# Softmax sums from a ones column beside each head's values, values loaded in single transfers, and an earlier rank for the splits of the normalised tile, in a one-core attention and two-layer MLP kernel

## The chip, the cores and the metric

One core of one Trainium2 chip runs the whole program in one launch. The metric is device microseconds (us), median of three runs. TensorE is called PE, VectorE DVE, ScalarE ACT, GpSimd POOL, and SP is the engine that issues most transfers.

## What is computed

The reference, cut to its steps (4 batches, 8 heads, 576 positions, 64 per head; 2304 tokens of 512 after the heads are joined):

```python
scores = scale * q @ k.T                       # causal window of 64 positions
attn = softmax(where(mask, scores, -1e9))
x = (attn @ v) joined over heads               # 2304 x 512
xn = x / rms(x) * rms_g
x = (silu(xn @ w_gate) * (xn @ w_val)) @ w_out # d_ff 1536
out = relu(x @ w_in)**2 @ w_out2               # d_ff 2048
```

## The kernel before

**Tiles.** The 2304 tokens are 36 blocks of 64 query positions, 9 to a batch. Block n looks at its own 64 keys and at the 64 before it. Heads go in four pairs, so a block's scores are four 128 x 128 tiles: on the partitions two heads' 64 queries, along the row 128 keys.

**Steps of a block** (`attention` and `block`). PE makes the scores (L430). DVE adds the mask and takes the row minimum (L435). ACT takes the exponential and, in the same instruction, the sum of each row (L437, `accum_out`). DVE turns the sum into its reciprocal (`den` L438, `rs` L439). PE transposes the four tiles into one PSUM bank (L443), ACT or DVE copies them to SBUF (`pt`), PE multiplies with the values (L453) into half of bank 7, DVE scales by `rs` into `acc` (L458), and ACT or DVE squares the result for the norm (L463 on ACT, L465 on DVE). Blocks go through in twos from the fifth on.

**Norm** (`rms`, once per four blocks). PE sums the squares (L479), a chain of nine tiny DVE instructions takes the reciprocal root, and for each block DVE scales `acc` into `xw` (L502), PE turns it by two transposes into half of bank 3 (L506), ACT or DVE copies the turned tile to the high part `xh` (a cast) and DVE takes the low part `xl` (L239, `R<-ps,R`). Copy and subtraction together are called the split of the tile here.

**Products.** All large products use high and low parts of both sides, so each is a run of matmuls at L608, L610 and L612. In the first stage the results go round a ring of three PSUM banks (`mm_ring`, banks 0 to 2), 256 columns each: two for the gate and value products of a feature group, four for the product that goes down. The second MLP (from 545 us, L820 and L884) works on its own banks. Weights arrive as 64-bit numbers and are decoded on ACT and DVE (L555 to L564).

**What sets the order.** Every step is handed to a list (`Schedule.add`) with its engine or two possible engines, a planned cost and a rank. `issue` goes through planned time and gives each engine, among the steps that are ready, the one of lowest rank. A step without a rank takes the lowest rank of what depends on it. A step with two engines goes to the second one only if that would end before the backlog of the first. Where PE's plan has a gap ahead of the first product, small filler matmuls are put in (`keep_busy`, L1015). The engines then run what stands in their queues, in that order, held only by semaphores; these are set per PSUM bank, not per half of a bank.

Of the kernel before, what the change touches and what calls it, by code (L numbers as in the profile page):

```python
# [9 lines left out]
F32 = mybir.dt.float32  # L10
# [6 lines left out]
ALU = mybir.AluOpType  # L17
# [28 lines left out]
PLACE = [5, 6, 1, 7, 2, 3, 4, 0, 8]  # L46
PN = 288
HALVES = 2
NPAIR = DFF2 // (2 * P)
# [4 lines left out]
ILEAD, ISTEP = 8.0, 2.0  # L54
ELEAD = 10.0
PORT, SHARED = 0.8, 1.0

class Schedule:
# [35 lines left out]
    def issue(self):  # L94
# [32 lines left out]
        for _ in range(n):  # L127
            skip = {}
            while True:
# [98 lines left out]
def attn_moe_moe2(ctx: ExitStack, tc: tile.TileContext, qT, kT, vw, w1, w2, w3, w4, rms_g, out):  # L228
# [78 lines left out]
    ps = [psum.tile([P, 512], F32, name=f"ps{i}") for i in range(8)]  # L307
    mm_ring = Ring([0, 1, 2])

# [11 lines left out]
    k_ring = ring(ap, "k", 2, [P, NP, (KB + 1) * WIN])  # L321
    v_ring = ring(ap, "v", 4, [P, DM])
# [3 lines left out]
    small = {k: ring(ap, k, 4, [P, NP]) for k in ("nb", "sum", "den", "rs")}  # L326
# [15 lines left out]
    def setup():  # L342
# [35 lines left out]

    k_tile = {}

    def load_keys(b, m, rank):

        k = k_ring.next()
        k0, k1 = max(KB * m - 1, 0) * WIN, KB * (m + 1) * WIN
        k_tile[b, m] = k, k0
        cuts = (0, WIN, 2 * WIN, k1) if (b, m) == (0, 0) else (k0, k1)
        for c0, c1 in zip(cuts, cuts[1:]):
            at("sp", 0.1 + (c1 - c0) / 110, lambda c0=c0, c1=c1: (nc.scalar if c0 < k0 + WIN and m == b == 0 else nc.sync).dma_start(out=T[k][:, :, c0 - k0 : c1 - k0], in_=kT[b, :, :, c0:c1]), w=[(k, c // WIN) for c in range(c0 - k0, c1 - k0, WIN)], lag=2.0)

    def attention(blocks, rank):  # L390

        todo = [block(n, rank, *more) for n, *more in blocks]
        for step in zip(*todo):
            if step[0][0] == "pe":

                costs, turn, fns, r, w, late = zip(*(x[1:] for x in step))
                at("pe", sum(costs) + turn[0], lambda fns=fns: [fn() for fn in fns], r=sum(r, []), w=sum(w, []), rank=rank + late[0])
            else:
                for x in step:
                    x[1]()  # L400

    def block(n, rank, part, pos):

        nk = WIN if n % NB == 0 else 2 * WIN
        b, i = divmod(n, NB)
        q, v, sm, pt = (r.next() for r in (q_ring, v_ring, sm_ring, pt_ring))
        nb, su, den, rs = (small[i].next() for i in ("nb", "sum", "den", "rs"))
        at("sp", 0.6, lambda: nc.sync.dma_start(out=T[q], in_=qT[n]), w=[q], lag=2.0)
        if i % KB == 0:
            load_keys(b, i // KB, rank)  # L410
        at("sp", 0.75, lambda: nc.sync.dma_start(out=T[v], in_=vw[n]), w=[v], lag=2.0)
        k, k0 = k_tile[b, i // KB]
        k0 = max(i - 1, 0) * WIN - k0
        keys_ = T[k][:, :, k0 : k0 + nk]
        kk = [(k, c // WIN) for c in range(k0, k0 + nk, WIN)]
        par = n % 2
# [3 lines left out]
        t_ps = ps[T_BANK].rearrange("p (a k) -> p a k", a=NP)  # L420
        x_ps = ps[X_BANK].rearrange("p (e a k) -> p e a k", e=2, a=NP)[:, par]
        sk = [("ps", c, par) for c in S_BANKS]
        xk = ("ps", X_BANK, par)

# [7 lines left out]
        def softmax():  # L432
# [15 lines left out]
        def pv():  # L448
            for i in range(2):
                for j in range(2):  # L450
                    for h in range(2):
                        f = (2 * i + h) * 2 * D + j * D
                        nc.tensor.matmul(x_ps[64 * h : 64 * h + 64, 2 * i + j], T[pt][:nk, 2 * i + j, 64 * h : 64 * h + 64], T[v][:nk, f : f + D], start=True, stop=True)  # L453
# [14 lines left out]

        return ("pe", 0.45, 0.28, scores, [q] + kk, sk, 0.0), ("", softmax), ("pe", 0.46, 0.24, pv, [v, pt], [xk], 0.02), ("", result)

# [3 lines left out]
    def rms(t, rank, part):  # L474
# [19 lines left out]
        for i, n in enumerate(blks(t)):  # L494
# [35 lines left out]
    def decode(srcs, rank=None, after=()):  # L530
# [9 lines left out]
        for z, src in zip(raws, srcs):  # L540
            sc.add("sp", 2.4 if closed2 else 1.5, lambda z=z, src=src: nc.sync.dma_start(out=T[z], in_=src), w=[z], lag=2.2, rank=rank, after=after)
        part = lambda i: T[raw].rearrange("p (a b) -> p a b", b=2)[:, :, i]
# [478 lines left out]
    def record(k):  # L1021
# [158 lines left out]
```

## Time and profile before

| | |
|---|---|
| median of three runs | 914.86 us (913.35 to 915.72) |
| the profiled execution's own time | 914.39 us |
| its span, first to last instruction | 912.70 us |
| PE busy | 894.8 us (98% of the span) |
| DVE, ACT, POOL busy | 698.0 (76%), 573.1 (63%), 42.7 us (5%) |
| granted PE clock | 1.0 of full speed (2.4 GHz) in every slice |

The profiled execution is 1.69 us longer than its span, and 0.47 us under the median. Shares over the whole span mix three stages: attention beside the first products (to about 114 us), products alone, and the second MLP.

### The profile page before, as it was taken

To read this page: it belongs to the slowest core of one execution; us is meant where nothing else is said; L and a number is where in the kernel's file an instruction comes from. 1 tells how busy PE (TensorE), PEld (TensorE's weight loads), DVE (VectorE), ACT (ScalarE), POOL (GpSimd) and SP (SyncE) were. 2 spreads that over 40 slices of the span, in tenths; PEclk is the share of its full clock that TensorE was granted. 3 is DMA by queue.
4 is the path that set the end of the run, shared out by engine and by line. 5 is a ranking of instruction groups with operands and counts; after the bars stand their busy time and mean duration, and the time that the engine had idled before them with its cause. 6 is when DMAs were issued, how large, how long until landed. Compare 5 with 4: busy or idle time off the path is not lost.

```text
span 912.7 us, 17324 instructions
## 1 busy us (share of the span) xinstructions
PE 894.8 (98%) x6598; PEld 839.3 (92%) x6598; DVE 698.0 (76%) x1663; ACT 573.1 (63%) x1227; POOL 42.7 (5%) x45
## 2 busy tenths in 40 slices
PE   7889999999999999999999999999999999999997
PEld 6778899989988988988988999999999999999997
DVE  5999987677767877777768558667789976777786
ACT  6998875666666667666667556655557655555561
POOL 1000000000000100000000000000002300000011
PEclk9999999999999999999999999999999999999999
DMA  8856520246535735534556136272717373718142
GB/s 248 267 180 216 164 87 2 93 163 240 181 109 179 239 124 179 204 113 169 189 199 231 56 115 211 79 249 75 267 57 270 106 269 107 274 51 288 36 169 98
DMA packets 67203, 149.50 MB, mean 164 GB/s; under 512 B 6704, under 2 KB 25136, under 8 KB 67120
## 3 DMA queue, kind: packets, MB, share of 16 engines
q1 hardware_dynamic: 66592, 148.26, 47.6%
q8 instruction: 52, 0.85, 0.4%
q14 instruction: 31, 0.25, 0.1%
q10 hardware_dynamic: 528, 0.13, 0.1%
HBM read 114.30 MB, written 34.08 MB: 163 GB/s over the span
## 4 chain that ended last, share of the span: by engine, by line
PE 86%; DVE 11%; DMA 1%; ACT 1%; issue 1%
PE ps L884 19%; PE ps L820 18%; PE ps L608 15%; PE ps L610 15%; PE ps L612 15%; DVE sm L435 2%; DVE R L239 1%; DVE Q L239 1%; DVE xw L502 1%; PE ps L453 1%; DVE acc L458 1%; PE ps L430 1%; PE ps L443 1%; PE ps L1015 1%; DMA Q<-w 1%
## 5 line engine op out<-in xcount | busy, mean ns | idle before, releaser
L820 PE MATMUL ps<-R 128*128 128x288 f32 x1344 | 187.5, 296 | 0.8 <-DVE ps L238 0.6
L820 PEld LDWEIGHTS ps<-R 128*128 128x128 f32 x1344 | 181.6, 189 | 1.8 <-DVE ps L238 0.8
L884 PE MATMUL ps<-L,R 128*128 128x288 f32 x630 | 169.7, 297 | 1.5 <-DVE acc L892 1.3
L884 PE MATMUL ps<-Q,L 128*128 128x288 f32 x480 | 133.4, 297 | 0.0
L884 PEld LDWEIGHTS ps<-L,R 128*128 128x128 f32 x630 | 118.6, 188 | 2.5 <-DVE acc L892 2.0
L608 PE MATMUL ps<-R 128*128 128x256 f32 (+3 forms) x444 | 99.8, 347 | 0.6 <-ACT R L238 0.6
L610 PE MATMUL ps<-R 128*128 128x256 f32 (+3 forms) x444 | 97.6, 342 | 0.0
L612 PE MATMUL ps<-R 128*128 128x256 f32 (+3 forms) x444 | 97.3, 341 | 0.0
L238 ACT CAST L<-Q 128x512 fp32r<-128x512 f32 (+3 forms) x104 | 57.3, 565 | 62.7 <-DVE Q L651 56.0
L892 DVE TENSOR_TENSOR acc<-ps,acc 128x288 f32<-128x288 f32 x136 | 61.5, 456 | 41.0 <-PE ps L884 38.5
L884 PEld LDWEIGHTS ps<-Q,L 128*128 128x128 f32 x480 | 90.7, 189 | 0.0
L608 PEld LDWEIGHTS ps<-R 128*128 128x128 f32 x444 | 75.1, 189 | 8.0 <-ACT R L238 0.7
L610 PEld LDWEIGHTS ps<-R 128*128 128x128 f32 x444 | 75.6, 189 | 6.6
L612 PEld LDWEIGHTS ps<-R 128*128 128x128 f32 x444 | 75.6, 189 | 6.6
L238 DVE COPY acc<-ps 128x448 f32<-128x448 f32 (+4 forms) x81 | 47.8, 590 | 38.6 <-PE ps L612 19.4
L651 DVE TENSOR_TENSOR Q<-ps,Q 128x512 f32<-128x512 f32 (+2 forms) x50 | 31.9, 638 | 59.1 <-PE ps L612 57.4
L238 ACT COPY acc<-ps 128x288 f32<-128x288 f32 (+4 forms) x108 | 47.3, 439 | 42.0 <-PE ps L884 27.4
L240 DVE TENSOR_TENSOR L<-Q,L 128x512 fp32r<-128x512 f32 (+2 forms) x94 | 71.0, 761 | 1.9 <-ACT L L238 1.8
L868 ACT CAST L<-Q 128x576 fp32r<-128x576 f32 (+1 forms) x45 | 33.9, 756 | 59.1 <-PE ps L884 59.0
L681 ACT COPY ps<-acc 128x448 f32<-128x448 f32 (+2 forms) x97 | 53.1, 554 | 23.3 <-DVE acc L238 21.4
L239 DVE TENSOR_TENSOR Q<-Q 128x288 f32<-128x288 f32 (+1 forms) x96 | 60.0, 625 | 3.5 <-ACT Q L833 0.4
L437 ACT ACTIVATE sm<-sm,nb 128x128 f32<-128x128 f32 (+1 forms) x144 | 55.4, 388 | 10.4 <-DVE nb L435 10.4
(124 smaller groups left out, 1722.4 us busy)
## 6 DMA issues: line engine op xcount, KB each, us to landing
Q<-w SPq DMA_DIRECT2D x68, 512.0 KB, 4.4
R<-su SPq DMA_DIRECT2D x16, 1024.0 KB, 6.1
su<-L SPq DMA_DIRECT2D x24, 512.0 KB, 3.2
sd<-L SPq DMA_DIRECT2D x24, 512.0 KB, 3.2
R<-su SPq DMA_DIRECT2D x16, 768.0 KB, 5.0
v<-vw SPq DMA_DIRECT2D x36, 256.0 KB, 3.8
R<-sd SPq DMA_DIRECT2D x8, 1024.0 KB, 5.7
L<-sd SPq DMA_DIRECT2D x8, 1024.0 KB, 7.7
```

The costliest lines, as they stand in the source:

```text
L238: copy = lambda e, out, in_: nc.scalar.copy(out, in_) if e == "act" else nc.vector.tensor_copy(out, in_)
L239: sub = lambda out, a, b: nc.vector.tensor_tensor(out, a, b, op=ALU.subtract)
L240: two = lambda e, out, a, b, op: (nc.vector if e == "dve" else nc.gpsimd).tensor_tensor(out, a, b, op=op)
L437: at("act", 0.39, lambda p=p: nc.scalar.activation(T[sm][:, p, :nk], T[sm][:, p, :nk], AF.Exp, bias=T[nb][:, p : p + 1], scale=-1.0, accum ...
L608: nc.tensor.matmul(acc, wh, xh, start=(i == 0 and not seeded), stop=False, skip_group_check=seeded)
L610: nc.tensor.matmul(acc, wl, xh, start=False, stop=False, skip_group_check=seeded)
L612: nc.tensor.matmul(acc, wh, xl, start=False, stop=(i == n - 1), skip_group_check=seeded)
L681: add("act", c_act(n), lambda b=b, dst=dst: nc.scalar.copy(ps[b][:, :n], dst), r=keys("acc", c, t), w=[("ps", b)])
L820: nc.tensor.matmul(bank, w_, x_, start=(start and i == 0), stop=(i == len(terms) - 1), skip_group_check=True)
L868: sc.add("act", c_act(m * PN), lambda z=z, o=o, m=m: nc.scalar.copy(z("h"), e(o, m)), r=ek(o, m), w=bk("h"))
L884: nc.tensor.matmul(bank, w_, x_, start=(start and i == 0), stop=(i == len(terms) - 1), skip_group_check=True)
L892: sc.add("dve", c_dve(PN), lambda: nc.vector.tensor_tensor(y(i, j), src, y(i, j), op=ALU.add), r=[key], w=yk(i, j))
```

## The change

- The value tile of a block is 8 x 65 wide: a column of ones stands beside each head's 64 values (set once by POOL). The product with the transposed scores is then 65 wide, and its last column is the softmax sum. `accum_out` goes from the exponential; `den` and `rs` are worked out behind that product, from PSUM. Two blocks at once no longer share bank 7: they use banks 7 and 2.
- So `mm_ring` loses bank 2. It now has four slots, the halves of banks 0 and 1.
- Transfers of queries, keys and values are listed by `load_inputs` ahead of the blocks' steps. The values of a block still come in one transfer, now in runs of 64 numbers. Blocks 2 to 7 load their second half only, and ACT copies the first half from the tile before (six copies of 64 x 520). The keys of the first six blocks come block by block.
- `rms`: copy and subtraction of the split get the rank of the norm step. In `Schedule.issue` the rule that kept an engine free for an urgent step goes, and until 100 us of planned time the second engine takes a step only if it is ahead by 0.4 us.

```diff
+VP = H * (D + 1)
+VHALVES = 8
+OPENING = 100.0, 0.4
...
-                    if ready_at[i] > t or (i not in self.urgent and soon(e, t + 0.7 * self.steps[i][1][engines.index(e)])):
+                    if ready_at[i] > t:
...
-                    if e == engines[0] or t + costs[1] + (SHARED if e == "pool" else 0.0) <= backlog(engines[0], i, t):
+                    if e == engines[0] or t + costs[1] + (SHARED if e == "pool" else OPENING[1] if t < OPENING[0] else 0.0) <= backlog(engines[0], i, t):
...
-    mm_ring = Ring([0, 1, 2])
+    for b in range(2):
+        ps += [ps[b][:, N1 * h : N1 * (h + 1)] for h in range(2)]
+        sc.names["ps", b] = [("ps", 8 + 2 * b + h) for h in range(2)]
+    mm_ring = Ring([8, 9, 10, 11])
...
-    S_BANKS, T_BANK, X_BANK, R_BANK = (4, 5), 6, 7, 3
+    S_BANKS, T_BANK, X_BANKS, R_BANK = (4, 5), 6, (7, 2), 3
...
+        for v in v_ring.slots:
+            at("pool", 0.2, lambda v=v: nc.gpsimd.memset(T[v].rearrange("p (c n) -> p c n", n=D + 1)[:, :, D:], 1.0), w=[(v, 1)])
...
+        for n in ns:
+            m = n + (n % NB == 0)
+            if m not in v_tile:
+                v = v_tile[m] = v_ring.next()
+                half = 1 < m < VHALVES
+                r = slice(WIN if half else 0, P)
+                at("sp", 0.7 if half else 1.4, lambda m=m, v=v, r=r: nc.sync.dma_start(out=heads(T[v][r]), in_=vw[m][r].rearrange("p (c n) -> p c n", n=D)), w=[(v, 2)] if half else [(v, 0), (v, 2)], lag=2.0)
+                if half:
+                    u = v_tile[m - 1]
+                    at("act", c_act(VP), lambda u=u, v=v: nc.scalar.copy(T[v][:WIN], T[u][WIN:]), r=[(u, 1), (u, 2)], w=[(v, 0)])
...
-                at("act", 0.39, lambda p=p: nc.scalar.activation(T[sm][:, p, :nk], T[sm][:, p, :nk], AF.Exp, bias=T[nb][:, p : p + 1], scale=-1.0, accum_out=T[su][:, p : p + 1]), r=[(nb, p)], w=[(sm, p), (su, p)])
-            at("dve", 0.07, lambda: nc.vector.tensor_scalar(T[den], T[su], 1e-9, None, op0=ALU.add), r=[(su, p) for p in range(NP)], w=[den])
-            at("dve", 0.09, lambda: nc.vector.reciprocal(T[rs], T[den]), r=[den], w=[rs])
+                at("act", 0.31, lambda p=p: nc.scalar.activation(T[sm][:, p, :nk], T[sm][:, p, :nk], AF.Exp, bias=T[nb][:, p : p + 1], scale=-1.0), r=[(nb, p)], w=[(sm, p)])
...
+            at("dve", 0.09, lambda: nc.vector.tensor_scalar(T[den], x_sum, 1e-9, None, op0=ALU.add), r=[xk], w=[den])
+            at("dve", 0.09, lambda: nc.vector.reciprocal(T[rs], T[den]), r=[den], w=[rs])
...
-            at(AD, c_ad(256, True), lambda e, xt=xt, hi=hi: copy(e, hi, xt), r=[pk], w=kk("xh"))
-            at("dve", c_dve(256), lambda xt=xt, hi=hi, lo=lo: sub(lo, xt, hi.bitcast(F32)), r=[pk] + kk("xh"), w=kk("xl"))
+            at(AD, c_ad(256, True), lambda e, xt=xt, hi=hi: copy(e, hi, xt), r=[pk], w=kk("xh"), rank=rank)
+            at("dve", c_dve(256), lambda xt=xt, hi=hi, lo=lo: sub(lo, xt, hi.bitcast(F32)), r=[pk] + kk("xh"), w=kk("xl"), rank=rank)
...
-            mm_ring.extend([3, 4])
+            mm_ring.slots, mm_ring.i = [2, 3, 4, 0, 1], 0
```

**DVE, the split of blocks 4 and 5** (the second norm). Before, in DVE's queue (ps_67 is bank 3, `xw` the scaled tile that PE turns next):

```order
L438 TENSOR_SCALAR den_121<-sum_117 128x4
L439 RECIPROCAL rs_123<-den_119 128x4
L238 CAST R<-ps_67 128x4x64
L502 SCALAR_TENSOR_TENSOR xw_109<-acc,r_131,gg 128x256
L239 TENSOR_TENSOR R<-ps_67,R 128x4x64
L502 SCALAR_TENSOR_TENSOR xw_110<-acc,r_131,gg 128x256
```

Now, at the same place (ps_71 is bank 7):

```order
L542 SCALAR_TENSOR_TENSOR xw_109<-acc,r_127,gg 128x256
L604 ISA Q<-Q 128x1024
L242 TENSOR_TENSOR R<-ps_67,R 128x4x64 x2
L542 SCALAR_TENSOR_TENSOR xw_110<-acc,r_127,gg 128x256
L242 TENSOR_TENSOR al_78<-s_75,ah_77 128x256
L496 TENSOR_SCALAR den_115<-ps_71 128x4
L242 TENSOR_TENSOR R<-Q,R 128x512
L497 RECIPROCAL rs_119<-den_115 128x4
```

The cast has gone to ACT, both subtractions stand together ahead of the second `xw`, and `den` and `rs`, which stood ahead of the split, now read the product's bank and come behind it.

**PE, a product that goes down, among the turns of the norm.** Before (ps0 to ps3 are banks 0 to 3; `ah`, `al` the activations, `xw` the tiles to be turned, `sm` the scores to be transposed):

```order
L612 MATMUL ps2_66<-al1_80,R_62 128x256
L612 MATMUL ps2_66<-al2_82,R_62 128x256
L506 MATMUL ps3_67<-ident_91,xw0_109 128x128 x2
L506 MATMUL ps3_67<-ident_91,xw1_110 128x128 x2
L443 MATMUL ps6_70<-ident_91,sm0_104 128x128 x4
L608 MATMUL ps0_64<-ah1_79,R_62 128x256
L608 MATMUL ps0_64<-ah2_81,R_62 128x256
```

Now:

```order
L652 MATMUL ps0_64<-al1_80,R_62 128x256
L652 MATMUL ps0_64<-al2_82,R_62 128x256
L546 MATMUL ps3_67<-ident_91,xw0_109 128x128 x2
L546 MATMUL ps3_67<-ident_91,xw1_110 128x128 x2
L648 MATMUL ps0_64<-ah1_79,R_62 128x256
L648 MATMUL ps0_64<-ah2_81,R_62 128x256
```

The second part of the product goes into the other half of bank 0, whose first half ACT or DVE is to read at that time; before, it went to another bank.

**ACT, the start of its queue.** Before (`sm` are the scores, `sum` the row sums):

```order
L437 ACTIVATE sm0_104,sum0_115<-sm0_104,nb0_111 128x64 x4
L437 ACTIVATE sm1_105,sum1_116<-sm1_105,nb1_112 128x128 x4
L437 ACTIVATE sm2_106,sum2_117<-sm2_106,nb2_113 128x128 x4
L437 ACTIVATE sm0_104,sum3_118<-sm0_104,nb3_114 128x128 x4
L555 ACTIVATE Q_63<-Q_63 128x1024
```

Now:

```order
L427 COPY v1_101<-v0_100 64x520
L477 ACTIVATE sm0_104<-sm0_104,nb0_111 128x64 x4
L427 COPY v2_102<-v1_101 64x520
L477 ACTIVATE sm1_105<-sm1_105,nb1_112 128x128 x2
L241 COPY pt0_107<-ps6_70 64x512
L477 ACTIVATE sm1_105<-sm1_105,nb1_112 128x128 x2
L477 ACTIVATE sm2_106<-sm2_106,nb2_113 128x128 x4
```

The first copy of values stands ahead of all exponentials, and the second ahead of block 1's; the first copy of transposed scores has come over from DVE.

## Rows read from the trace of the kernel before

**Rows 1.** The page, part 1: busy us, share of the span, instructions.

```profile
PE 894.8 (98%) x6598; PEld 839.3 (92%) x6598; DVE 698.0 (76%) x1663; ACT 573.1 (63%) x1227; POOL 42.7 (5%) x45
```

**Rows 2.** Windows: stretch, length, then each engine's busy us; last PE clock, DMA share, GB/s.

```profile
4.48:24.00 19.52, 18.55 (x244) 15.56 (x248) 14.09 (x77) 13.92 (x54) 0.00 (x0) 1.00 0.86 263
24.00:34.00 10.00, 8.71 (x136) 7.41 (x135) 9.93 (x47) 9.06 (x33) 0.00 (x0) 1.00 0.83 286
...
34.00:114.00 80.00, 74.60 (x1079) 66.97 (x1078) 79.00 (x407) 70.54 (x259) 0.00 (x0) 1.00 0.64 198
114.00:540.00 426.00, 426.00 (x2423) 384.78 (x2422) 309.58 (x609) 273.71 (x480) 18.66 (x18) 1.00 0.44 150
540.00:912.70 372.70, 366.96 (x2727) 364.62 (x2725) 285.43 (x529) 204.56 (x404) 21.00 (x12) 1.00 0.47 164
```

**Rows 3.** Waits of PE from 24 to 114 us: total us, times, longest.

```profile
PE ps L506 <- DVE R L239: 3.9, 6, 0.8
PE ps L506 <- DVE xw L502: 1.2, 2, 0.8
PE ps L608 <- ACT R L238: 0.6, 1, 0.6
```

**Rows 4.** Timeline around 50 us: start, length, instruction, idle ahead of it.

```profile
49.06 0.42 DVE L239 TENSOR_TENSOR R<-ps,R 128x256 fp32r<-128x256 f32 x1
...
49.41 0.48 DVE L502 SCALAR_TENSOR_TENSOR xw<-acc,r,gg 128x256 f32<-128x256 f32 x1
49.80 0.42 DVE L239 TENSOR_TENSOR R<-ps,R 128x256 fp32r<-128x256 f32 x1
...
50.27 0.66 PE L506 MATMUL ps<-ident,xw 128*128 128x128 f32 x4 [0.75 <-DVE R L239]
```

**Rows 5.** Groups by line, 0 to 140 us: DVE (busy us, mean ns).

```profile
L465 DVE CUSTOM_DVE_ANT_1 R<-acc 128x256 fp32r<-128x256 f32 x16 | 6.7, 423 | 0.0
...
L238 DVE COPY pt<-ps 128x512 f32<-128x512 f32 (+1 forms) x8 | 5.5, 689 | 1.5 <-PE ps L443 1.5
...
L563 DVE TENSOR_SCALAR Q<-Q 128x1024 uint32<-128x1024 uint32 (+1 forms) x7 | 4.3, 614 | 0.0
...
L238 DVE CAST R<-ps 128x256 fp32r<-128x256 f32 x10 | 4.2, 420 | 0.0
...
L238 DVE COPY acc<-ps 128x256 f32<-128x256 f32 x7 | 2.9, 420 | 0.0
```

**Rows 6.** The same groups: PE and ACT.

```profile
L443 PE MATMUL ps<-ident,sm 128*128 128x128 f32 (+1 forms) x140 | 22.3, 283 | 0.4 <-ACT pt L238 0.4
...
L453 PE MATMUL ps<-v,pt 128*64 128x64 f32 (+1 forms) x544 | 20.6, 226 | 0.7 <-DVE acc L458 0.4 <-DVE pt L238 0.2
...
L238 ACT COPY pt<-ps 128x512 f32<-128x512 f32 (+1 forms) x26 | 15.0, 576 | 2.6 <-PE ps L443 2.2
...
L1015 PE MATMUL ps<-ident 128*128 128x128 f32 x68 | 11.7, 313 | 0.0
...
L463 ACT ACTIVATE R<-acc 128x256 fp32r<-128x256 f32 x16 | 6.6, 414 | 2.0 <-DVE acc L458 1.8
```

**Rows 7.** Timeline of two exponentials of block 1 on ACT.

```profile
9.03 0.39 ACT L437 ACTIVATE sm<-sm,nb 128x128 f32<-128x128 f32 x1
...
9.32 0.18 ACT L437 ACTIVATION_READ_ACCUMULATOR sm<-sm,nb 128x1 f32 x1
9.42 0.39 ACT L437 ACTIVATE sm<-sm,nb 128x128 f32<-128x128 f32 x1
```

**Rows 8.** Transfers issued to 40 us: KB each, median us to landing.

```profile
v<-vw SPq DMA_DIRECT2D x12, 256.0 KB, 4.1
...
q<-qT SPq DMA_DIRECT2D x15, 128.0 KB, 4.1
...
k<-kT SPq DMA_DIRECT2D x2, 128.0 KB, 3.8
```

**Rows 9.** The page, part 5: the up product of the second MLP.

```profile
L820 PE MATMUL ps<-R 128*128 128x288 f32 x1344 | 187.5, 296 | 0.8 <-DVE ps L238 0.6
```

**Rows 10.** Timeline near 631 us: an urgent copy from bank to bank.

```profile
631.08 0.38 ACT L238 COPY ps<-ps 128x288 f32<-128x288 f32 x1 [1.41 <-PE ps L820]
```

More of the change, by code (lines that the diff above doesn't have):

```diff
@@ L321, in attn_moe_moe2 @@
     k_ring = ring(ap, "k", 2, [P, NP, (KB + 1) * WIN])
-    v_ring = ring(ap, "v", 4, [P, DM])
+    v_ring = ring(ap, "v", 4, [P, VP])
     sm_ring = ring(ap, "sm", 3, [P, NP, P])
@@ L325, in attn_moe_moe2 @@
     xw_ring = ring(ap, "xw", 2, [P, NP * WIN])
-    small = {k: ring(ap, k, 4, [P, NP]) for k in ("nb", "sum", "den", "rs")}
+    small = {k: ring(ap, k, 4, [P, NP]) for k in ("nb", "den", "rs")}
     small["part"] = ring(ap, "part", 3, [P, 8])
     small["r"] = ring(ap, "r", 2, [P, 3, 8])
-    S_BANKS, T_BANK, X_BANK, R_BANK = (4, 5), 6, 7, 3
+    S_BANKS, T_BANK, X_BANKS, R_BANK = (4, 5), 6, (7, 2), 3
     attn_steps, first_steps = [], []
@@ L376, in setup, with load_keys, part @@
         at("act", 0.3, lambda: nc.scalar.copy(T["gg"], gp.rearrange("p i (j d) -> p (i j) d", j=2)), r=[("ps", R_BANK, 0)], w=["gg"])
-    k_tile = {}
-    def load_keys(b, m, rank):
+    k_tile, k_part = {}, {}
+    def load_keys(b, m):
         k = k_ring.next()
-        k0, k1 = max(KB * m - 1, 0) * WIN, KB * (m + 1) * WIN
+        k0, k1 = max(KB * m - 1, 0), KB * (m + 1)
         k_tile[b, m] = k, k0
-        cuts = (0, WIN, 2 * WIN, k1) if (b, m) == (0, 0) else (k0, k1)
-        for c0, c1 in zip(cuts, cuts[1:]):
-            at("sp", 0.1 + (c1 - c0) / 110, lambda c0=c0, c1=c1: (nc.scalar if c0 < k0 + WIN and m == b == 0 else nc.sync).dma_start(out=T[k][:, :, c0 - k0 : c1 - k0], in_=kT[b, :, :, c0:c1]), w=[(k, c // WIN) for c in range(c0 - k0, c1 - k0, WIN)], lag=2.0)
+        def part(c0, c1):
+            at("sp", 0.5 * (c1 - c0), lambda: (nc.scalar if c0 == b == 0 else nc.sync).dma_start(out=T[k][:, :, (c0 - k0) * WIN : (c1 - k0) * WIN], in_=kT[b, :, :, c0 * WIN : c1 * WIN]), w=[(k, c - k0) for c in range(c0, c1)], lag=2.0)
+        k_part[b, m] = part, k0, k1
+        return part, k0, k1
@@ new lines, in attn_moe_moe2, with load_inputs @@
+    inputs, v_tile = {}, {}
+    heads = lambda a: a.rearrange("p (c n) -> p c n", n=D + 1)[:, :, :D]
+    def load_inputs(ns):
+        for n in ns:
+            b, i = divmod(n, NB)
+            q = q_ring.next()
+            at("sp", 0.5, lambda n=n, q=q: nc.sync.dma_start(out=T[q], in_=qT[n]), w=[q], lag=2.0)
+            inputs[n] = [q]
+            if i % KB == 0:
+                part, c0, c1 = load_keys(b, i // KB)
+                if n >= 2 * KB:
+                    part(c0, c1)
+            if n < 2 * KB:
+                part, c0, _ = k_part[0, n // KB]
+                part(max(n - (n == KB), 0), n + 1)
+        for n in ns:
+            m = n + (n % NB == 0)
[7 more added lines that the diff above has]
+                    at("act", c_act(VP), lambda u=u, v=v: nc.scalar.copy(T[v][:WIN], T[u][WIN:]), r=[(u, 1), (u, 2)], w=[(v, 0)])
+            inputs[n].append(v_tile[m])
@@ L390, in attention @@
     def attention(blocks, rank):
+        load_inputs([x[0] for x in blocks])
         todo = [block(n, rank, *more) for n, *more in blocks]
@@ L405, in block @@
         b, i = divmod(n, NB)
[L406 to L411, printed above, removed]
+        q, v = inputs[n]
+        sm, pt = (r.next() for r in (sm_ring, pt_ring))
+        nb, den, rs = (small[i].next() for i in ("nb", "den", "rs"))
         k, k0 = k_tile[b, i // KB]
-        k0 = max(i - 1, 0) * WIN - k0
-        keys_ = T[k][:, :, k0 : k0 + nk]
-        kk = [(k, c // WIN) for c in range(k0, k0 + nk, WIN)]
+        k0 = max(i - 1, 0) - k0
+        keys_ = T[k][:, :, k0 * WIN : k0 * WIN + nk]
+        kk = [(k, c) for c in range(k0, k0 + nk // WIN)]
         par = n % 2
@@ L420, in block @@
         t_ps = ps[T_BANK].rearrange("p (a k) -> p a k", a=NP)
-        x_ps = ps[X_BANK].rearrange("p (e a k) -> p e a k", e=2, a=NP)[:, par]
+        x_bank = ps[X_BANKS[par]]
+        x_ps = x_bank[:, : NP * (D + 1)].rearrange("p (a n) -> p a n", a=NP)
+        x_sum, x_ps = x_ps[:, :, D], x_ps[:, :, :D]
         sk = [("ps", c, par) for c in S_BANKS]
-        xk = ("ps", X_BANK, par)
+        xk = ("ps", X_BANKS[par])
         def scores():
@@ L451, in pv @@
                     for h in range(2):
-                        f = (2 * i + h) * 2 * D + j * D
-                        nc.tensor.matmul(x_ps[64 * h : 64 * h + 64, 2 * i + j], T[pt][:nk, 2 * i + j, 64 * h : 64 * h + 64], T[v][:nk, f : f + D], start=True, stop=True)
+                        f, o = ((2 * i + h) * 2 + j) * (D + 1), (2 * i + j) * (D + 1)
+                        nc.tensor.matmul(x_bank[64 * h : 64 * h + 64, o : o + D + 1], T[pt][:nk, 2 * i + j, 64 * h : 64 * h + 64], T[v][:nk, f : f + D + 1], start=True, stop=True)
         def result():
             x = T["acc"][:, :, n * WIN : (n + 1) * WIN]
+            at("dve", 0.09, lambda: nc.vector.tensor_scalar(T[den], x_sum, 1e-9, None, op0=ALU.add), r=[xk], w=[den])
+            at("dve", 0.09, lambda: nc.vector.reciprocal(T[rs], T[den]), r=[den], w=[rs])
             at("dve", c_dve(256), lambda: nc.vector.tensor_tensor(x, x_ps, T[rs].unsqueeze(2).to_broadcast([P, NP, WIN]), op=ALU.mult), r=[xk, rs], w=allk("acc", (n, 1)))
@@ L467, in result @@
             at(AD, (c_act(256) + 0.19, c_dve(256) + 0.085), squares, r=allk("acc", (n, 1)), w=allk("xl", (n, 1)) + [(part, pos)])
-        return ("pe", 0.45, 0.28, scores, [q] + kk, sk, 0.0), ("", softmax), ("pe", 0.46, 0.24, pv, [v, pt], [xk], 0.02), ("", result)
+        return ("pe", 0.45, 0.28, scores, [q] + kk, sk, 0.0), ("", softmax), ("pe", 0.47, 0.24, pv, [(v, 0), (v, 1), (v, 2), pt], [xk], 0.02), ("", result)
     half = [0]
@@ L540, in decode @@
         for z, src in zip(raws, srcs):
-            sc.add("sp", 2.4 if closed2 else 1.5, lambda z=z, src=src: nc.sync.dma_start(out=T[z], in_=src), w=[z], lag=2.2, rank=rank, after=after)
+            sc.add("sp", 2.4 if closed2 else 1.9, lambda z=z, src=src: nc.sync.dma_start(out=T[z], in_=src), w=[z], lag=2.2, rank=rank, after=after)
         part = lambda i: T[raw].rearrange("p (a b) -> p a b", b=2)[:, :, i]
```

## The prediction

> **What bounds the kernel now.** I read the page's part 1 first: PE is busy for 894.8 of 912.70 us [rows 1], so the time is PE's work plus the gaps in it, and a change that leaves PE's work alone can win the gaps at most. Then the windows, to see where the gaps are [rows 2]. From 114 to 540 us there is none: 426.00 of 426.00 us. From 540 us on PE is busy for 366.96 of 372.70 us, so 5.74 us are open there. The rest lies in the opening, where attention runs beside the first products. From 24 to 114 us PE is busy for 8.71 + 74.60 = 83.31 of 90 us, which leaves 6.69 us. DVE in the same 90 us is busy for 9.93 + 79.00 = 88.93 us: it is the bound there, and ACT with 9.06 + 70.54 = 79.60 us comes next.
>
> The waits say what PE misses [rows 3]: of the 6.69 us, 3.9 + 1.2 = 5.1 us in eight waits are those of the turning of the normalised tiles (L506), for the subtraction of an earlier split (six times, up to 0.8 us) or for the scaled tile. One of them can be followed on the timeline [rows 4]: the first subtraction begins at 49.06 us, DVE then scales a tile, the second subtraction begins at 49.80, and PE, open since 0.75 us, turns the next tile at 50.27. What DVE does late in the opening, PE does late, and since PE has no gap from 114 to 540 us every us won there is won at the end.
>
> **DVE's load.** I counted the instructions in the two programs' queues up to the last `den`, since the planner moves work that the diff doesn't name. DVE loses 8 squares, 7 casts of the split, 7 copies to `acc`, 2 copies of transposed scores and one weight cast, and gets 3 decode steps of 1024 while it loses one of 512. With the means of [rows 5]: 8 x 0.423 + 14 x 0.420 + 2 x 0.689 = 10.6 us less, 3 x 0.614 = 1.8 us more, so 8.8 us less of 88.93. (The weight cast and the short decode step are left out; they would add to the saving.) `den` and `rs` stay 36 each and only change their place. The 144 row minima with their mask stay.
>
> **ACT's load.** It gets that work, and is paid by the sums: behind each exponential stands a read of the accumulator, which begins at 9.32 us, and the next exponential begins at 9.42 [rows 7]. So the sum costs 0.10 us each, 14.4 us for 144. Against it: 8 squares x 0.414, 9 casts and 6 copies of 256 from PSUM at no more than 0.414, one copy of scores at 0.576 and six copies of values, 520 long like the 512 of a copy of scores, at 0.576 [rows 6]: 9.5 + 4.0 = 13.5 us. Decode steps go over to DVE (three of 1024), which leaves ACT at or a little under what it has now.
>
> **The sum,** in us, against the profiled execution's 914.39 (its span of 912.70 and 1.69 around it).
>
> Gaps of the opening. DVE with 8.8 us less would need 80.1 us where PE's work needs 83.3, so PE would become the bound of these 90 us and the whole 6.69 us could go; with DVE 4% behind, gaps from bursts stay. The subtractions standing together and ahead of the next tile are the direct cure for the wait of [rows 4]. Bounds: 0 (if ACT or PE's own waits take DVE's place) to -6.7. I take -5.6, the L506 waits and 0.5 of the others.
>
> Fillers ahead of the first product: 37 instead of 34. 34 of them are 68 passes and 11.7 us [rows 6], 0.34 each. Bounds 0 (they stand where PE would wait anyway) to +1.0; I take +0.8.
>
> The product with values is 65 wide instead of 64: 20.6 us of matmuls [rows 6], 1/64 of it is 0.3 at most, 0 if the loading of weights paces it. I take +0.1.
>
> The start. ACT's first instruction is now a copy of values ahead of block 0's exponentials, 0.58 us by [rows 6], and the second one stands ahead of block 1's. Against it, six transfers of values are halved while the DMA engines are 0.86 busy [rows 2]. Bounds -0.6 to +1.2, take +0.3.
>
> Half banks. Semaphores go by bank. In the new queues I find 32 places where the first matmul of a product must wait for an instruction that reads the other half of its bank, all before the first stage ends; in the queues of before there is none in this ring. At 20 of them PE has, by the matmuls that stand between and their durations, over 2 us of other work, enough for one reader of 0.42 us [rows 5] behind two others. At 12 it has less, at five only a group of transposes: 35 groups take 22.3 us [rows 6], 0.64 us, against a copy of 0.42 and the semaphores around it. Bounds 0 to 12 x 0.42 = +5.0. I take 0.2 at the five and 0.2 for the others together: +1.2.
>
> The runs of 64 numbers in the transfers of values: the profile has such runs, in the two key transfers of 64 columns, which land after 3.8 us, while queries of the same 128 KB in long rows take 4.1 [rows 8]. I take 0; the other bound is one landing, 4.1, if the first values came that much later, and no run here yet shows the whole 256 KB in that form. The Trainium skill, "DMA: Bandwidth & Descriptors", section Specifications, asks for runs of at least 512 bytes for full rate; in these rows runs of 256 bytes are not slower.
>
> The later stages. The rule that kept an engine free for the urgent copy from bank to bank has gone, and seven of the 32 such copies are now on DVE instead of one. In the order two groups of six matmuls stand between the product that is copied and the one that needs the copy; a matmul there takes 187.5 / 1344 = 0.14 us [rows 9], so there are 1.7 us for a copy of 0.38 us [rows 10] with, in the order, up to two others ahead of it on its queue. I take 0, bounds -1 to +1.5, since the order of squares and copies after 540 us also changes a little.
>
> Sum: -5.6 + 0.8 + 0.1 + 0.3 + 1.2 = -3.2, so **911.2 us**, 0.4% under the median of 914.86 that the runs show (0.47 of that is the profiled execution's own distance from the median).
>
> **Rivals.** First, ACT takes DVE's place, no change. For it: ACT is at 79.60 of 90 us already, and half banks hold it up too. In the new order 7 tanh and 11 copies on ACT must wait for the last matmul into the other half, a group of 12 or 6 matmuls. At 0.14 x 256/288 = 0.124 us each [rows 9] that is 7 x 1.5 + 11 x 0.75 = 18.7 us, of which I put two thirds before 114 us, by where they stand among the attention steps, about as much as ACT has open (10.4). Against it: part of these waits falls where ACT waits anyway. Price: of the 5.6 us about 1.4 stay won, and 914.39 - 1.4 + 2.4 gives 915.4, or with half the gain 912.6; I call it 914.
>
> Second, slower: the half banks become PE's longest wait. For it: the bank of the normalised tiles is shared by halves already, and six of the waits in [rows 3] are of just this sort, the turn into one half held by the subtraction that reads the other, 3.9 us in six, 0.65 each. If the 32 new places cost what these cost, they cost 20.8 us; the 12 tight ones alone 7.8. With the gain of 5.6, 2.0 for what is left of the costs (fillers, width, start, other places) and 7.8 the time is 918.6. It decides from about 0.55 us at each of the 12. Against it: at most of the places the reader is ACT, which is not the full engine, and half of the places lie after 114 us, where neither ACT nor DVE is full. The Trainium skill has the rule behind it: "PSUM — Partial Sum Buffer", section PSUM bank collisions raise a hardware error, says to guard PSUM by bank and quadrant, not by address. The trace agrees, as far as the waits of the shared bank show it. By that rule alone, at the row's 0.65 for each tight place, one is at 918.6; by the readers' durations at 911.2.
>
> Third, values in short runs arrive late: if each landing took 4.1 us longer, the first product with values would come that much later while DVE goes on with the other blocks; half of it shows, and 911.2 + 2.1 gives 913.3.
>
> **How the numbers follow.** 0.3%, about what a measurement of this kernel can tell from no change, is 2.7 us, so faster is under 912.1 and slower over 917.6. The forecast has 0.53 (its own range 908.0 to 912.1), ACT in DVE's place 0.25 and late values 0.07 (both within 0.3%: 0.32), the half banks 0.15. The low end is the sum with all 6.7 us won and the half banks and fillers almost free, 908; the high end, 917, goes into the slow case, of which some two thirds and a few hundredths below 908 are left out, under 0.2.
>
> **What the new profile would show.** Right: the waits of the turning for the subtraction at 1.5 us or less in the opening; DVE below 95% there and PE above 96%; no row of the accumulator read behind an exponential; waits of a product for a reader of its bank of 0.6 us at most each; 114 to 540 us without a gap. Wrong: ACT full where DVE was and PE waiting for scores or `pt`; waits of L648 for L241, L694 or L695 that sum to over 3 us; a longer wait of the first value product for its transfer; gaps after 540 us of clearly more than 5.7 us.

## The result and the profile after

The changed kernel takes 919.88 us in the median (918.44 to 922.21, 4 runs), before beside it 914.59 (913.35 to 915.72, 4 runs): 1.006 times as long, 95% interval 1.0043 to 1.0076. Run again beside later experiments it took 919.55 us (6 runs; 1.0049, 1.0035 to 1.0063). The forecast was 911.2 us and faster. The profiled execution took 918.44 us, 4.05 us more than that of before, with a span of 916.7 us.

The page's part 1 after, which answers to [rows 1]:

```profile
PE 895.9 (98%) x6604; PEld 839.6 (92%) x6604; DVE 685.9 (75%) x1625; ACT 576.2 (63%) x1128; POOL 49.9 (5%) x53
```

DVE lost 12.1 us of work and PE gained 1.1 us. So of the 4.05 us some 3 are gaps of PE. The windows of after say where, against [rows 2]:

```profile
4.48:24.00 19.52, 17.98 (x257) 15.52 (x257) 12.76 (x74) 18.03 (x44) 0.00 (x0) 1.00 1.00 254
24.00:34.00 10.00, 7.32 (x102) 5.90 (x101) 8.38 (x46) 8.51 (x22) 0.00 (x0) 1.00 0.95 241
34.00:114.00 80.00, 75.60 (x1095) 69.13 (x1096) 75.46 (x386) 67.39 (x200) 0.00 (x0) 1.00 0.68 185
114.00:540.00 426.00, 423.38 (x2394) 380.10 (x2393) 297.71 (x586) 276.61 (x462) 20.32 (x20) 1.00 0.44 149
540.00:916.70 376.70, 370.71 (x2747) 368.12 (x2745) 291.54 (x539) 205.72 (x403) 26.39 (x14) 1.00 0.47 163
```

From 24 to 114 us PE is open for 90 - 82.92 = 7.08 us, where it was 6.69. DVE is busy for 83.84 us of them, where it was 88.93: its saving is there, and PE got nothing of it. From 114 to 540 us, where before had no gap, 426.00 - 423.38 = 2.62 us are open. After 540 us it is 5.99 against 5.74. Against that, PE's first matmul begins 0.94 us sooner (3.54 against 4.48 us).

What PE, ACT and DVE wait for from 24 to 175 us, in after (total us, times, longest):

```profile
ACT s L693 <- PE ps L652: 15.6, 10, 2.3
DVE s L694 <- ACT s L693: 11.9, 7, 3.5
...
PE ps L546 <- DVE xw L542: 1.9, 2, 1.7
...
PE ps L648 <- DVE s L695: 1.6, 3, 0.6
...
PE ps L481 <- ACT pt L241: 1.5, 2, 1.2
...
PE ps L648 <- ACT acc L241: 1.4, 3, 0.5
PE ps L546 <- DVE R L242: 1.2, 4, 0.5
...
PE ps L648 <- DVE s L694: 0.8, 1, 0.8
```

and the two longest of these kinds in before, the same stretch:

```profile
ACT s L653 <- PE ps L612: 6.1, 8, 1.1
...
DVE s L654 <- ACT s L653: 3.1, 4, 1.3
```

The waits in front of the turns (L546) fell from the 5.1 us of [rows 3] to 3.1. In their place stand seven waits of products (L648) for readers in their ring of banks, 1.6 + 1.4 + 0.8 = 3.8 us, of which before had one, of another kind (0.6 us). The larger numbers are those of ACT and DVE: the tanh (L693) waits 15.6 us for products, before 6.1, and DVE's first multiplication behind it (L694) waits 11.9 us for the tanh, before 3.1. The second is 8.8 us more; that the forecast let DVE save just this number is chance.

One such place in after, on the timeline (start, length, instruction, idle ahead of it). The first product of a pair ends at 149.94 us, the second one begins at 149.92:

```profile
149.54 0.40 PE L652 MATMUL ps<-R 128*128 128x256 f32 x2
...
149.92 0.72 PE L648 MATMUL ps<-R 128*128 128x256 f32 x4
...
150.96 0.64 PE L652 MATMUL ps<-R 128*128 128x256 f32 x4
151.44 0.40 PE L648 MATMUL ps<-ah,R 128*128 128x256 f32 x2
...
151.70 0.38 ACT L693 ACTIVATE s<-ps 128x256 f32<-128x256 f32 x1 [2.30 <-PE ps L652]
...
152.12 0.42 DVE L694 SCALAR_TENSOR_TENSOR s<-s,ps 128x256 f32<-128x256 f32 x1 [1.85 <-ACT s L693]
...
153.13 0.41 DVE L695 SCALAR_TENSOR_TENSOR s<-s,ps 128x256 f32<-128x256 f32 x1
...
153.60 0.50 PE L648 MATMUL ps<-ah,R 128*128 128x256 f32 x2 [0.56 <-DVE s L695]
```

The tanh reads the first product, complete at 149.94, and ACT has nothing else to do for 2.30 us; it begins at 151.70, 0.10 us after the second product's last matmul (151.60), which went into the other half of the bank. Both multiplications come late by that, DVE meanwhile puts four small steps of the norm between them, and the third product down, which by the ring's order needs the half that the tanh and the first multiplication have read by 152.54, waits for the second multiplication, the reader of the other half. So 1.76 us late on an engine that has time become 0.56 us on PE, and 0.1 more: the first two matmuls behind the wait take 0.50 us where the same two at 151.44 take 0.40, which counts as busy. From 113 us on seven of ten tanh begin 1.5 to 1.8 us behind their own product and within 0.1 us of the end of the second; in before all ten begin within 0.1 us of their own.

### The profile page after: what moved, and what is told of

It reads as the page before. It is cut to its first block, busy times and chain, and to the rows that moved or that the text cites. A ratio compares the mean times of both kernels' runs of the same rounds, so it can differ in the third digit from the quotient of the medians.

```text
span 916.7 us, 17208 instructions
## 1 busy us (share of the span) xinstructions
PE 895.9 (98%) x6604; PEld 839.6 (92%) x6604; DVE 685.9 (75%) x1625; ACT 576.2 (63%) x1128; POOL 49.9 (5%) x53
## 4 chain that ended last, share of the span: by engine, by line
PE 85%; DVE 10%; ACT 2%; DMA 1%; issue 1%; SPq 1%; DVEq 0%; ACTq 0%
PE ps L860 18%; PE ps L924 18%; PE ps L648 16%; PE ps L650 15%; PE ps L652 15%; DVE Q L242 1%; DVE sm L475 1%; DVE R L242 1%; DVE xw L542 1%; PE ps L491 1%; DMA Q<-w 1%; DMA g<-rms_g 1%; DVE acc L498 1%; PE ps L470 1%; ACT sm L477 0%
## 5 line engine op out<-in xcount | busy, mean ns | idle before, releaser
L648 PE MATMUL ps<-R 128*128 128x256 f32 (+3 forms) x444 | 99.5, 346 | 0.8 <-DVE s L694 0.8
L241 ACT CAST L<-Q 128x512 fp32r<-128x512 f32 (+3 forms) x106 | 58.1, 566 | 53.5 <-DVE Q L691 48.1
L648 PEld LDWEIGHTS ps<-R 128*128 128x128 f32 x444 | 75.1, 188 | 8.6 <-DVE s L694 1.2
L241 ACT COPY acc<-ps 128x288 f32<-128x288 f32 (+4 forms) x113 | 49.2, 438 | 50.3 <-PE ps L924 24.4
L241 DVE COPY acc<-ps 128x448 f32<-128x448 f32 (+4 forms) x76 | 45.2, 596 | 40.5 <-PE ps L652 20.3
L243 DVE TENSOR_TENSOR L<-Q,L 128x512 fp32r<-128x512 f32 (+3 forms) x94 | 71.1, 765 | 2.7 <-ACT L L241 2.4
L241 ACT COPY Q<-ps 128x288 f32<-128x288 f32 x84 | 33.4, 398 | 37.7 <-PE ps L860 37.2
```

Of the source, the lines that this page charges most:

```text
L241: copy = lambda e, out, in_: nc.scalar.copy(out, in_) if e == "act" else nc.vector.tensor_copy(out, in_)
L243: two = lambda e, out, a, b, op: (nc.vector if e == "dve" else nc.gpsimd).tensor_tensor(out, a, b, op=op)
L648: nc.tensor.matmul(acc, wh, xh, start=(i == 0 and not seeded), stop=False, skip_group_check=seeded)
```

## The experiments

Theories: **banks** (the half banks make readers and products wait for each other; the rest gains or is neutral), against **transfers** (short runs make weights and keys late), **ACT** (it is full in DVE's place) and **plan** (the planner's new rules lose the time). Each kernel was timed beside before, whose medians were 914.33 to 914.49 us there. An interval given is of the ratio to before.

**Values in rows of 65 in memory.** The ones stand in the input array, and a row goes over in one run. The order on every engine is after's.

```diff
-    ... dma_start(out=heads(T[v][r]), in_=vw[m][r].rearrange("p (c n) -> p c n", n=D))
+    ... dma_start(out=T[v][r], in_=vw[m][r])
```

> After, with the values laid out in memory in rows of 65 with the one in place, so that each row of 520 numbers goes over in one run of 2080 bytes instead of eight of 256; every engine's order stays as it is in after. If short runs are what keeps w and k late (DVE waits 1.5 us at 26.8 for a w, PE 0.6 and 0.8 us at 10.4 and 17.5 for k), those waits go and the PE's 1.65 us wait for xw at 29.0 with them: 916.5 to 918 us. If the transfers' bytes or their order do it, or the waits come from elsewhere: 919 to 920.5 us, with the same waits.

918.86 us (1.0035 to 1.0061). PE's waits for transfers of keys up to 24 us in after:

```profile
PE ps L470 <- DMA k<-kT: 4.9, 3, 3.5
```

Its transfers issued up to 40 us (KB each, median us to landing):

```profile
v<-vw SPq DMA_DIRECT2D x5, 256.0 KB, 3.9
...
k<-kT ACTq DMA_DIRECT2D x1, 128.0 KB, 2.7
```

The waits with long runs:

```profile
PE ps L470 <- DMA k<-kT: 4.9, 1, 4.9
```

and the transfers with them:

```profile
v<-vw SPq DMA_DIRECT2D x5, 260.0 KB, 3.5
...
k<-kT ACTq DMA_DIRECT2D x1, 128.0 KB, 4.0
```

The two later waits for keys (4.9 - 3.5 = 1.4 us) went, as the transfers theory has it, but the first one grew by as much: the first keys land after 4.0 us instead of 2.7 when a value transfer of long runs stands beside them. The wait for `xw` at 29 us shrank from 1.65 to 1.19, and did not go. The time lies between the two ranges that were expected: by the medians 1 us of the loss is the short runs', and the intervals of the two kernels overlap.

**Half banks in turn.** Only the ring's order changes, so that the two products of a pair stand in different banks.

```diff
-    mm_ring = Ring([8, 9, 10, 11])
+    mm_ring = Ring([8, 10, 9, 11])
```

> After, with the four half banks taken in the order bank 0, bank 1, bank 0, bank 1, so that the two products of one pair stand in different banks. Half-bank theory: the tanh of a pair's first product no longer waits until the second product's last matmul, its readers come about 1 us sooner, and the seven waits of L648 (3.75 us between 55 and 174 us) fall below 1.5 us: 917 to 918 us. If a late DVE or ACT makes these waits, whatever bank they read: the same waits, 919.5 to 920.5 us.

917.03 us (1.0023 to 1.0050). The tanh's part came as the banks theory has it; the pair of 149.94, now on this timeline:

```profile
147.26 0.64 PE L652 MATMUL ps<-R 128*128 128x256 f32 x4
...
148.00 0.38 ACT L693 ACTIVATE s<-ps 128x256 f32<-128x256 f32 x1 [0.64 <-PE ps L652]
...
148.92 0.64 PE L652 MATMUL ps<-R 128*128 128x256 f32 x4
```

It begins 0.10 us behind its own product and 1.56 ahead of the second one's end, and so do nine of the ten after 113 us. But the expectation for L648 failed: its waits are 3.8 us again, now at other products. The time is the one expected, for another reason: in this order the turns wait 1.9 us instead of 3.1 and the sums of squares (L519) not at all instead of 1.1. Which half shares a bank with which moves the waits of products; it doesn't take them away.

**Half banks alone, in before.** Four halves of banks 0 and 1 for the three full banks, bank 2 empty.

```diff
-    mm_ring = Ring([0, 1, 2])
+    mm_ring = Ring([8, 9, 10, 11])
```

> Before, with the products of the first stage in four half banks (banks 0 and 1, in after's order) in place of three full banks; bank 2 stands empty until the ring grows, nothing else is changed. Half-bank theory: waits of L608 of 2.5 to 4 us in sum appear before 180 us, 917 to 918.5 us. If the half banks cost what was forecast (1.2 us) or nothing: 914.5 to 916 us.

925.09 us (1.0108 to 1.0138): three times what even the banks theory expected. Its two runs at a mean granted clock of 1.0 took 924.39 and 924.49 us, so a lower clock is not the cause. From 24 to 175 us, where before's DVE waited 3.1 us for the tanh and 2.3 for products:

```profile
DVE s L657 <- PE ps L615: 8.5, 4, 3.0
...
PE ps L509 <- DVE R L239: 5.0, 5, 1.8
...
DVE s L657 <- ACT s L656: 4.1, 3, 1.6
```

DVE, full in before, stands for up to 3.0 us behind a first multiplication that waits for the other half's product, and the turns that PE needs stand in the queue behind it.

**No copies of values on ACT.**

```diff
-VHALVES = 8
+VHALVES = 0
```

> After, with the whole 128 rows of values loaded for the first blocks too, so that the six copies of value halves on ACT (0.6 us each) go and six transfers are 256 KB instead of 128. If a full ACT is what makes PE wait (pt, 1.5 us in the opening): 917 to 918.5 us. If the transfers are what is short in the first 30 us: w and k later still, 920 to 922 us. If neither: 919 to 920.5 us.

918.17 us (1.0029 to 1.0053), 1.7 less than after. Taken by itself it speaks for ACT. On another order, further down, the same edit costs 3.4 us.

**The planner of after in before,** and **the planner of before in after:** ranks of the splits, the rule for urgent steps, `OPENING` and the cost of a weight transfer, as the change's diff has them, the one way and the other.

> Before, with the planner of after alone: ranks on the splits, no engine kept free for urgent steps, 0.4 us asked for before DVE takes ACT's work in the first 100 us, 1.9 us for a weight transfer. Banks, sums and values stay as in before. If the planner part is sound and the half banks are what turned the change: L506's waits (5.1 us) fall by 2 us or more, 911.5 to 913.5 us. If the new plan itself loses time: 915 to 918 us.

> After, with the planner of before: no ranks on the splits, engines kept free for urgent steps, no price on DVE's help, 1.5 us for a weight transfer. Half-bank theory, with what half banks did to before under this plan (10.7 us): 919 to 924 us. If the new plan is what loses time in after: 915 to 917.5 us.

Before with the new planner: 915.22 us (1.0000 to 1.0021), no gain, and just inside what the plan theory expected. The waits of the turns fell by more than 2 us as the other theory has it (5.1 to 2.2), but its eleven runs have mean granted clocks of 0.994 to 0.998, before's beside it 0.999 or 1.0; the last section shows what that costs. After with the old one: 925.35 us (1.0107 to 1.0138), as the banks theory has it and a little over. So the new rules alone don't gain, and beside half banks they are worth 5.5 us.

**After without the column of ones.** Sums from the exponentials' accumulators, values in one bank and in full rows, three full banks; loads and planner stay after's.

```diff
-    mm_ring = Ring([8, 9, 10, 11])
+    mm_ring = Ring([0, 1, 2])
...
-    S_BANKS, T_BANK, X_BANKS, R_BANK = (4, 5), 6, (7, 2), 3
+    S_BANKS, T_BANK, X_BANK, R_BANK = (4, 5), 6, 7, 3
```

> After without the column of ones: the sums come from the exps' accumulators again, values in one bank and in long runs, the first products in three full banks as in before; the halves of values loaded once, the order of the loads and the planner stay as in after. Half-bank theory: no tanh waits for the other product of its pair after 113 us (seven did, by 1.5 us each), waits of L648 below 1 us, 912 to 915 us. If the loads or the plan make the loss: 918 us or more.

**912.45 us** (0.9972 to 0.9989), faster than before. No wait of a product is left in its list from 24 to 175 us:

```profile
DVE s L691 <- ACT s L690: 4.3, 4, 2.5
...
PE ps L543 <- DVE R L242: 1.9, 3, 0.7
...
PE ps L480 <- ACT pt L241: 1.2, 2, 0.9
...
PE ps L543 <- DVE xw L539: 0.8, 2, 0.5
...
PE ps L467 <- DVE nb L472: 0.8, 1, 0.8
```

So the ones, with their banks and the short runs that come with them, cost about 7 us (1.006 against 0.998 of before), and everything else in the change gains 1.9.

**A planner that knows the shared banks.** All of after stays. A product isn't issued before the readers of its bank that are ahead of it are through, a reader not before the products that are, by planned times; the steps are otherwise the same.

```diff
+        self.bank[i] = {(k[1] - 8) // 2 for k in r + w if k[0] == "ps" and 8 <= k[1] < 12}
...
-                    if ready_at[i] > t:
+                    if max([ready_at[i]] + [(read if e == "pe" else written)[b] for b in self.bank[i]]) > t:
...
+            for b in self.bank[i]:
+                x = written if e == "pe" else read
+                x[b] = max(x[b], t + cost + lag)
```

> After, with a planner that knows that the two halves of a bank wait for each other: a product isn't issued before the readers of the other half that stand ahead of it are done, and a reader not before the products that stand ahead of it. If the loss is work that stands in DVE's and ACT's queues behind such a waiting reader (DVE waits 11.9 us for the tanh, 3.1 in before): these waits fall by half, 915.5 to 917.5 us. If the waits come from banks too few, whatever the order: 919 to 921 us.

> Before with four half banks (925.1 us), and a planner that knows that the halves of a bank wait for each other; nothing else changes. If the 10.7 us came from work queued behind readers that wait for the other half, most of it goes: 914.5 to 918 us, DVE's waits for the products (8.5 us) fall below 3 us. If four halves of two banks are simply too few beside three full banks: 921 us or more.

After with it: 913.42 us (0.9980 to 1.0001), 6 us less, better than expected. PE's and DVE's waits from 24 to 175 us:

```profile
DVE s L699 <- ACT s L698: 4.0, 4, 1.8
...
PE ps L551 <- DVE R L247: 2.3, 5, 0.9
...
PE ps L551 <- DVE xw L547: 1.6, 2, 1.4
...
PE ps L486 <- ACT pt L246: 1.5, 2, 1.2
```

DVE's wait for the tanh is 4.0 us instead of 11.9, and products wait for nobody. Before with half banks (925.09) and this planner: **915.18 us** (1.0000 to 1.0017), 9.9 of the 10.7 us back, and

```profile
DVE s L662 <- ACT s L661: 6.7, 4, 2.4
```

with 0.4 us in all of waits of DVE's multiplications for products, where they were 8.5 and more. DVE's wait for the tanh is even longer than without the planner (4.1), so that wait by itself doesn't set the time. Both have the same four halves. So it isn't their number that costs: it is work that an order made for four free slots puts in the queues behind a reader or a product that can't go yet.

**On top of it:** long runs of values; with these, the first value transfer two places later on SP's queue; with this, no copies on ACT.

> The planner that knows the banks, with the values in rows of 65 in memory (runs of 2080 bytes); the order on every engine is that of the run before it. Runs of 256 bytes delay what lands after 10 us: with long runs the waits for k at 10.7 and 18.4 us (1.0 us) and part of DVE's 2.2 us for w go. But the first product starts later, as it did with long runs alone (4.86 us against 3.54), since the first k lands later beside a value transfer of long runs. Transfers theory: the two cancel, 912.5 to 914 us. If long runs only gain: 911 to 912.5 us.

> The same, with the first value transfer issued two places later on SP's queue, behind the next q and k. If the first k lands late because the values' long runs stand beside it, it lands near 3.5 us again, the first product starts 0.8 to 1.3 us sooner and the sum is 911.5 to 913 us. If the start hangs on something else (k's own issue): the first product stays at 4.6 to 4.9 us and the time that of the run before.

> The same as the run before, with all 128 rows of values loaded for the first blocks, so without the six copies of halves on ACT (3.7 us of its time before 40 us), and 0.8 MB more to transfer. If the full ACT of the first 50 us still makes PE wait (pt: 1.5 us): 910.5 to 912 us. If the transfers are the shorter cover there: 913 us or more.

913.01 us (0.9971 to 0.9988), 914.22 (0.9987 to 1.0004) and 917.66 (1.0027 to 1.0053). The long runs change little, as the transfers theory expected. Later values bring the first matmul from 4.93 to 4.24 us, a little less than expected, PE then waits 0.76 us for the next keys, and the time rises where a fall was expected. Without the copies it is 3.4 us longer, as expected if the transfers are the shorter cover (913 us or more), where the same edit in after had given 1.7, as expected if ACT is full. About 1 us of the 3.4 goes with the clock: its one run at a mean clock of 1.0 took 916.75 us, the other eight, at 0.996 or 0.998, 917.32 to 920.11. The last two edits each make another order of the opening, and which part of 1.2 and 3.4 us is the order's isn't shown; that the copies gain or cost can't be said from these runs.

**All shared banks known,** those of scores and turns too: after with long runs, and after without the ones.

> After with long value runs and a planner that knows the sharing in the banks of the scores and of the turns too, beside the products' (913.0 us with the products' alone). If the waits that are left in front of the turns (L551, 4.6 us) have the same cause, they fall by 1.5 us or more: 910.5 to 912.5 us. If not: 912.5 to 915 us.

> After without the column of ones (912.45 us), with the planner that knows the sharing of the banks of scores, values and turns. If those banks hold hidden waits as the halves did: 910 to 911.8 us. If not: 912 to 914 us.

913.21 us (0.9978 to 0.9996) and 913.22 (0.9979 to 0.9996): no gain on 913.01 and 912.45. The first one's turns did lose waits (L551: 2.1 us instead of 4.6), but PE then waits as long elsewhere. The two also show the column of ones at its best, without the cost of its banks: equal.

**After once more.**

> After itself once more, beside these runs. Both theories: 919 to 921 us; in runs with a granted clock below 1.0 one or two microseconds more than in those at 1.0, and the same seven waits of L648 (3.75 us).

919.55 us, with the same seven waits of L648 (3.8 us) and DVE's 11.9 us. What was expected of the clock failed: the three runs at 1.0 took 917.87, 919.33 and 920.19 us, the three below it 918.88, 919.76 and 920.05.

## Why the prediction was wrong

**Two terms of the sum failed: the half banks' +1.2 and the gaps of the opening, -5.6.** By the medians the change is 5.3 us slower than before, where the sum said 3.2 faster, a miss of 8.5. After with the planner that knows the banks, where no product waits for a reader any more, is 0.9 faster (913.42 against 914.33), where the sum without the half banks' term said 4.4. After without the ones is 1.9 faster, where it has no half banks at all. So the half banks cost some 6 to 7 us instead of 1.2, and the other terms miss by 2.5 to 3.5. (Both experiments also change the rest of the order, so the parting is rough.)

**Half banks, +1.2.** The step took 32 places where a product waits for a reader of the other half; it put the reader's 0.42 us there and set PE's other work against it. It took for granted that the reader begins when its product is done. The runs show that it doesn't: it waits for the second product as well, 1.5 to 1.8 us, and takes DVE's next steps with it. The prediction did count these waits, seven tanh of 1.5 us, which is just what the trace has; but it set them against ACT's open time only (first rival), two thirds of them before 114 us (all seven are after 113), and never asked what stands behind the tanh on DVE. Removing the ones with their banks gives 7 us, telling the planner of the banks 6.

**The second rival came true;** it had said 918.6 us: 7 tight places at 0.54 us each, where it said that it decides from about 0.55 at 12. Its price was right by two errors, so by luck: the visible waits of products are 3.8 us instead of 7.8, and the gain that it took off, 5.6, is not there. Its sign came, waits of L648 for L241, L694 or L695 of over 3 us in sum. The rule that it cited, of the Trainium skill ("PSUM — Partial Sum Buffer", section PSUM bank collisions raise a hardware error), has engines that touch one bank kept apart by semaphores, whichever of its columns they use. The trace agrees: the kernel's semaphores hold the tanh until 151.70 us, though its own half is complete at 149.94.

**Gaps of the opening, -5.6.** DVE's load fell (98.8% to 93.2% of the 90 us, "below 95%" was right) and the L506 waits fell, by 2.0 us instead of 5.1. PE's gaps there grew by 0.4. 1.65 us of the turns' 3.1 are one wait for `xw` at 29.04 us, behind DVE's 1.5 us for a weight transfer. PE came to 92.1%, not "above 96%". Nor were the half banks all that kept the 5.6 us away. These are the windows of after with the planner that knows the banks:

```profile
24.00:34.00 10.00, 8.10 (x119) 6.54 (x110) 8.66 (x45) 8.80 (x22) 0.00 (x0) 1.00 1.03 261
34.00:114.00 80.00, 76.25 (x1106) 69.91 (x1106) 76.93 (x397) 69.85 (x206) 0.00 (x0) 1.00 0.71 191
114.00:540.00 426.00, 425.86 (x2413) 384.23 (x2413) 303.74 (x592) 273.86 (x456) 19.64 (x20) 1.00 0.44 150
```

The gap after 114 us is gone but for 0.14 us, while from 24 to 114 us PE is still open for 90 - 84.35 = 5.65 us, 1.04 less than before, with DVE busy for 85.59. Without the ones it is 5.11 us, 1.58 less. The step that failed is the one from DVE's load to PE's gaps: DVE has idle time there, and the turns wait all the same for a single subtraction or scaled tile (3.9 us in the list of that planner's run), and PE for one `pt`.

**ACT's load** is right: no accumulator read stands behind an exponential, the exponentials follow each other by 0.29 us instead of 0.39 (seven take 2.15 us from 10.13 us on), and ACT is busy for 75.9 of the 90 us, 79.6 before. It isn't full; it waits. The first rival is not borne out, but for one wait for `pt` of 1.2 us. (Its price has a slip: with half the gain, 914.39 - 2.8 + 2.4 is 914.0 and not 912.6.)

**Width and fillers:** 225 ns a product with values instead of 226, within the bounds, and 37 groups of fillers in 11.3 us instead of 34 in 11.7, which is 0.4 less, where the step had 0 to 1.0 more: its mean of 0.34 a group did not hold.

**The start, +0.3:** the first matmul comes 0.94 us sooner, and the two new waits for keys take 1.4. So the start costs about 0.5 us: the number is near, by luck, since the mechanism (copies on ACT) wasn't it.

**Short runs, 0:** right for the landing that the step spoke of (3.9 us for 256 KB), blind for the transfers beside it. From 4.48 to 24 us the DMA engines are busy for 1.00 of the time, with long runs for

```profile
4.48:24.00 19.52, 18.89 (x269) 16.20 (x269) 12.15 (x69) 15.96 (x41) 0.00 (x0) 1.00 0.87 241
```

0.87. The Trainium skill, "DMA: Bandwidth & Descriptors", section Specifications, wants 512 bytes or more for full rate, and these shares agree with it; all the same it is worth about 1 us here.

**Later stages, 0:** the gaps after 540 us grew by 0.25 us, within the bounds.

What stays open: the 6 to 7 us are more than the 3.8 us of waits that PE shows for products. Between the spans of after and of after with the planner that knows the banks (916.7 and 911.2) lie 5.5 us; by their windows 3.7 of these are gaps of PE (20.77 against 17.05 us) and 1.8 its busy time (895.93 against 894.15). Seven times the 0.1 us more behind the wait at 153.60 would be 0.7 of the second, an estimate; the rest isn't taken apart. Nor is a best version settled: 912.45 us without the ones and 913.01 with them, long runs and the planner that knows the banks, both beat before by 0.2%, and their intervals overlap.

## What to carry to other kernels

When buffers are made smaller than the unit that the semaphores guard (here halves of a PSUM bank), count the wait of the reader too, and follow it into the queue that stands behind it: a stall on an engine with spare time costs by what is queued behind it. Tell a planner of every such shared unit before judging the buffers; here that turned +10.7 us into +0.7 with the same four slots. A load taken off a full engine brings nothing where the engine then spends the time waiting, so read its waits and not only its busy time.

## What the runs showed of the hardware

**The clock can fall in the opening.** Windows of the experiment with halves in turn (behind POOL's busy time stands the granted clock):

```profile
48.00:52.00 4.00, 2.17 (x17) 1.43 (x14) 4.00 (x20) 3.76 (x15) 0.00 (x0) 1.00 0.49 131
52.00:56.00 4.00, 4.00 (x44) 3.74 (x44) 3.08 (x15) 3.09 (x10) 0.00 (x0) 0.57 0.02 4
```

and of the one with long runs and the planner that knows the banks:

```profile
26.00:30.00 4.00, 1.78 (x30) 1.38 (x26) 2.07 (x12) 2.65 (x7) 0.00 (x0) 0.98 0.78 224
30.00:33.00 3.00, 2.81 (x38) 2.37 (x39) 2.15 (x9) 2.67 (x7) 0.00 (x0) 0.50 0.77 244
```

PE had been busy for 2.17 and 1.78 of 4 us; then, with PE nearly full, the clock was at the lower of its two levels, 1.2 GHz. The same 32 matmuls of scores behind that wait take 1.56 us there and 0.90 with the same order, short runs and no drop. After's own profile shows none, so its 4.05 us owe nothing to it; but two of its four runs have a mean clock of 0.998, among them the slowest one (922.21). In the runs of before with the new planner the time goes with the mean clock: six at 0.998 took 914.02 to 915.22 us, three at 0.996 915.87 to 916.57, two at 0.994 917.34 and 917.61. In those of after it doesn't show. A gap in the opening can so cost more than its length.

**A transfer's landing goes with its neighbours:** the first 128 KB of keys took 2.7 us beside a value transfer in runs of 256 bytes (after, after once more, and the planner that knows the banks), and 3.9 to 4.1 us beside one in runs of 2080 (three kernels). With the value transfer issued two places later it took 3.4 us. In before, whose values also come in long runs, it took 3.6 us, so the run length is not all of it.
